# Windowed attention and feed-forward: probabilities transposed in blocks on VectorE and moved through DRAM, from the third batch on

## The chip, the core and the metric

The kernel runs on one core of a Trainium2 chip. The metric is the device time of one execution in microseconds. Five things work side by side on the core, each with an in-order queue of its own: TensorE (PE, matmuls, with its weight loads PEld), VectorE (DVE), ScalarE (ACT), GpSimd (POOL) and SyncE (SP), which issues every transfer of this kernel. A transfer is carried out by 16 shared DMA engines after SP has issued it.

## The reference, cut to what matters

```python
batch, n_heads, seq_l, seq_g, head_dim = (8, 8, 512, 32, 64)
# attention, per batch and head: 32 global queries see all 544 keys; each of the 512 local
# queries sees the 32 global keys and the local keys at most 32 positions away
s_g = scale * np.matmul(q_g, k_all.transpose(0, 1, 3, 2))
out_g = np.matmul(sm(s_g), v_all)
mask = np.abs(pos[:, None] - pos[None, :]) <= window        # window = 32
s_l = np.concatenate([s_lg, np.where(mask, s_ll, -1e9)], axis=-1)
out_l = np.matmul(sm(s_l), np.concatenate([v_g, v_l], axis=2))
x = concatenate([out_g, out_l], axis=2), heads side by side  # 8 * 544 = 4352 rows of 512
h = x @ w_in                                                 # 512 x 2048
return (h - np.tanh(h)) @ w_out                              # 2048 x 512
```

All inputs and outputs are float32.

## The kernel before, in words

**Precision.** From the second batch on every operand of a matmul is split in a rounded part and a rest (`thi` and `tlo` for the transposed probabilities, `vv` for the values, `x_hi` and `x_lo`, `ghi` and `glo`, and so on), and a product is made of the three products hi·hi, hi·lo and lo·hi. The first part of each such pair is a copy (ACT or DVE), the second a subtraction, mostly on POOL (`subtract`).

**Attention.** A head's 512 local queries are four tiles of 128; a tile needs 192 local and 32 global keys (`KC = 224`). Tiles go in two pairs. Per pair: scores into a PSUM bank (lines 733 and 734), the row's peak with the mask (738, DVE), exponential (745, ACT), reciprocal of the sum (752, 753, DVE), scaling (758, POOL) in the buffers `prob`. The product with the values needs the keys on the partitions, so each pair's probabilities are transposed on PE in four 128x128 pieces against the identity `idr` (line 918) into a PSUM bank, from which `add_keys_first` writes `thi` (line 291, ACT or DVE) and `tlo` (line 836, DVE). The product itself is line 916: eight matmuls for a pair from the third batch on (`wide`, `CFG["newb"] = 2`), four with 128 and four with 64 weight columns, twelve in the second batch. The transposes of head i are issued inside the product of head i-1, one after each quarter of it (`add_product(pair, then)`). `thi` and `tlo` exist once: head i's writes come after head i-1's product has read them.

After the product its two halves are added (`low`, line 947), and `x_hi`, `x_lo` (953, POOL) and the global rows `xg` (957) are made.

The global queries' probabilities `pg` take another way already: 32x32 blocks transposed on DVE (line 789) into `gt`, then `thi` and `tlo` (801).

**Feed-forward.** A batch's 512 local rows are one chunk of 16 steps. A step is 12 matmuls of 512 columns for the hidden layer (line 1014), tanh (1022, ACT), difference (1025, DVE), split (`ghi` line 291, `glo` line 1031 on POOL), and 12 matmuls for the output (1062). The chunk of batch b-1 runs while batch b's attention is made, two steps for a head. `x_hi` and `x_lo` exist twice, so attention is never more than a batch ahead. After the last head the last batch's chunk and one of the 256 global rows remain.

**Order.** The class `Order` lays every operation on its engine's queue at build time: a list scheduler with a price for each operation, due times (the numbers in `CFG`), and choices such as "this copy on ACT or on DVE". The queues on the chip are in order, so an operation that waits holds all behind it.

**Transfers.** For each head SP issues four loads of keys and queries (551), four moves of the keys to the score operand `kw` (646), two of the queries (651) and three loads of values (855, 866); for each batch also ten for the global keys and queries and four of the output (1090).

## Time and profile before

| | |
|---|---|
| median of three runs | 1089.13 us (1078.9 to 1089.97) |
| the profiled execution, its own time | 1082.97 us |
| span of the profile, first to last instruction | 1081.2 us |
| mean granted TensorE clock | 0.987 of full speed |
| busy: PE, DVE, ACT, POOL | 95%, 64%, 58%, 61% of the span |
| bytes moved by the DMA engines | 97.10 MB |

The span is 1.8 us shorter than the execution's own time. Busy shares are of the whole span. The program has stages: the first two batches (0 to some 221 us, with the weights being loaded and split), six batches of attention beside the feed-forward of the batch before (221 to 934 us), and a tail of feed-forward alone. A busy PE is not a PE at its peak, since matmuls overlap in the record: the pace is read from the starts of successive matmuls. Times in the lists are us from the start of the span; "idle before" is time in which the engine stood still ahead of an instruction, with what released it. Releasers named with a small q are sequencers; SPq rows are SP issuing a transfer.

### The profile page before, as it was taken

Reading aid. Unit: us, or ns where it says so; the run is one execution under the profiler, and the core shown is the slowest. Engines: PE = TensorE matmul, PEld = TensorE weight load, DVE = VectorE, ACT = ScalarE, POOL = GpSimd, SP = SyncE. Lnnn points to the kernel's source line nnn. Section 1 sums busy time; section 2 is a strip of 40 time slices with the busy share of each in tenths; the row PEclk is TensorE's granted clock in tenths of the full one; section 3 lists DMA queues with packets and bytes.
Section 4 is the critical chain, followed back from the end, with each engine's and each line's share of the span. In section 5 each row is a group of like instructions: output and inputs, shape, how many; then the busy total and the mean of one; then the engine's idle time right before and its main releaser. Section 6 shows DMA issues by size and latency. Waiting matters only on the chain.

```text
span 1081.2 us, 19499 instructions
## 1 busy us (share of the span) xinstructions
PE 1022.2 (95%) x5660; PEld 858.0 (79%) x5660; DVE 695.3 (64%) x2167; ACT 630.7 (58%) x1764; POOL 659.1 (61%) x912
## 2 busy tenths in 40 slices
PE   5987999879999899999999999999999999999997
PEld 3765878668888788878888888878888888888896
DVE  5786877777676776677666776677757776422221
ACT  4776767557674766576665766477647666311111
POOL 4556767567675677577666776677756776522221
PEclk9998999889999999999999999999999999999999
DMA  7655545454334532353334433353335331000010
GB/s 180 154 138 152 148 119 153 113 139 93 70 82 86 134 83 64 68 137 84 78 67 114 92 84 79 75 138 79 76 66 140 84 79 45 16 24 1 1 40 20
DMA packets 270795, 97.10 MB, mean 90 GB/s; under 512 B 217312, under 2 KB 255072, under 8 KB 270688
## 3 DMA queue, kind: packets, MB, share of 16 engines
q1 hardware_dynamic: 270688, 95.86, 38.5%
q8 instruction: 45, 0.74, 0.3%
q14 instruction: 62, 0.51, 0.2%
HBM read 49.27 MB, written 8.91 MB: 54 GB/s over the span
## 4 chain that ended last, share of the span: by engine, by line
PE 82%; DMA 4%; DVE 4%; issue 3%; POOL 2%; SPq 2%; ACT 1%; POOLq 0%; DVEq 0%; ACTq 0%
PE bank L1014 33%; PE bank L1062 32%; PE bank L916 6%; PE bank L918 4%; PE bank L733 3%; PE bank L734 2%; DMA wraw<-in_moe_w_out_dram 2%; DMA lo<-lo 2%; SPq L551 1%; PE bank L676 1%; PE bank L730 1%; DVE gt L789 1%; PE bank L677 0%; DVE t L1025 0%; POOL w_out_lo L372 0%
## 5 line engine op out<-in xcount | busy, mean ns | idle before, releaser
L1031 POOL TENSOR_TENSOR glo<-t,ghi 128x512 fp32r<-128x512 f32 x136 | 176.0, 1294 | 174.7 <-DVE ghi L291 82.3
L1022 ACT ACTIVATE t<-bank 128x512 f32<-128x512 f32 x136 | 81.4, 598 | 159.5 <-PE bank L1014 154.3
L1025 DVE TENSOR_TENSOR t<-bank,t 128x512 f32<-128x512 f32 x136 | 93.9, 690 | 120.5 <-ACT t L1022 117.9
L1062 PE MATMUL bank<-w_out_hi,ghi 128*128 128x512 f32 x544 | 155.0, 399 | 4.1 <-ACT ghi L291 4.1
L1062 PE MATMUL bank<-w_out_lo,ghi 128*128 128x512 f32 x544 | 154.9, 399 | 0.0
L1062 PE MATMUL bank<-w_out_hi,glo 128*128 128x512 f32 x544 | 154.4, 397 | 0.4 <-POOL glo L1031 0.4
L1014 PE MATMUL bank<-x_lo,w_in_hi 128*128 128x512 f32 x512 | 142.4, 400 | 0.0
L1014 PE MATMUL bank<-x_hi,w_in_hi 128*128 128x512 f32 x512 | 141.8, 401 | 0.0
L1014 PE MATMUL bank<-x_hi,w_in_lo 128*128 128x512 f32 x512 | 140.9, 397 | 0.0
L758 POOL TENSOR_SCALAR prob<-prob,st 128x224 f32<-128x224 f32 x240 | 107.2, 460 | 37.1 <-DVE st L753 21.8
L745 ACT ACTIVATE prob<-prob,st 128x224 f32<-128x224 f32 x240 | 113.7, 476 | 21.1 <-DVE st L738 19.8
L1062 PEld LDWEIGHTS bank<-w_out_hi,ghi 128*128 128x128 f32 x544 | 100.9, 190 | 25.8 <-ACT ghi L291 5.4
L738 DVE CUSTOM_DVE_ANT_0 prob<-bank,mask 128x224 f32<-128x224 f32 x240 | 83.2, 388 | 56.0 <-PE bank L734 53.1
L918 PE MATMUL bank<-idr,prob 128*128 128x128 f32 x440 | 116.8, 282 | 1.8 <-DVE xg L977 1.0
L916 PE MATMUL bank<-thi,vv 128*128 128x160 f32 (+5 forms) x512 | 118.3, 286 | 0.0
L1062 PEld LDWEIGHTS bank<-w_out_lo,ghi 128*128 128x128 f32 x544 | 100.3, 190 | 19.3
L1062 PEld LDWEIGHTS bank<-w_out_hi,glo 128*128 128x128 f32 x544 | 99.2, 189 | 20.3 <-POOL glo L1031 1.3
L1014 PEld LDWEIGHTS bank<-x_hi,w_in_hi 128*128 128x128 f32 x512 | 95.5, 192 | 21.3 <-ACT x_hi L291 0.6
L953 POOL TENSOR_TENSOR x_lo<-wraw,x_hi 64x256 fp32r<-64x256 f32 x96 | 70.8, 738 | 60.3 <-ACT x_hi L291 33.9
L1014 PEld LDWEIGHTS bank<-x_lo,w_in_hi 128*128 128x128 f32 x512 | 93.5, 191 | 17.6
L1014 PEld LDWEIGHTS bank<-x_hi,w_in_lo 128*128 128x128 f32 x512 | 92.6, 190 | 17.0
L916 PE MATMUL bank<-tlo,vv 128*64 128x160 f32 x448 | 104.2, 233 | 0.0
(132 smaller groups left out, 2057.9 us busy)
## 6 DMA issues: line engine op xcount, KB each, us to landing
wraw<-in_moe_w_in_dram SPq DMA_DIRECT2D x32, 256.0 KB, 3.0
wraw<-in_moe_w_out_dram SPq DMA_DIRECT2D x32, 256.0 KB, 3.1
out_dram<-wraw SPq DMA_DIRECT2D x32, 256.0 KB, 2.3
vraw<-in_v_l_dram SPq DMA_DIRECT2D x56, 128.0 KB, 2.4
raw<-in_k_l_dram SPq DMA_DIRECT2D x112, 64.0 KB, 2.3
raw<-in_q_l_dram SPq DMA_DIRECT2D x112, 64.0 KB, 2.3
hi<-hi SPq DMA_DIRECT2D x56, 128.0 KB, 2.3
lo<-lo SPq DMA_DIRECT2D x56, 128.0 KB, 2.3
```

Of the source, the lines that this page charges most:

```text
L733: nc.tensor.matmul(t_[:, i, :KC], part_lo[:, q], kw2[:, t], start=True, stop=False)
L738: nc.vector.tensor_tensor_reduce(out=self.prob[t][:, :KC], in0=getattr(self, f"s_{pair}")[:, i, :KC], in1=tile_mask[t], scale=-0.125, scal ...
L745: nc.scalar.activation(x, x, AF.Exp, bias=self.st[:, t:t + 1], scale=-1.0, accum_out=self.st[:, 4 + t:5 + t])
L758: nc.gpsimd.tensor_scalar(x, x, self.st[:, 8 + t:9 + t], 1.0, op0=ALU.mult, op1=ALU.mult)
L916: nc.tensor.matmul(dst, l, r, start=i == 0, stop=i == len(mm) - 1, skip_group_check=True)
L918: nc.tensor.transpose(*turns[i // each], idn)
L953: eng[e].tensor_sub(places()[1], view(total, [(160, 2), (1, P)]), f32(places()[0]))
L1014: nc.tensor.matmul(self.h[s][:, j * n:(j + 1) * n], w[:, cc, f * P:(f + 1) * P], self.x()[xi][:, cc, :n], start=part == 0 and cc == 0 and ...
L1022: nc.scalar.activation(tt_[q], self.h[s], AF.Tanh)
L1025: nc.vector.tensor_sub(tt_[q], self.h.pop(s), tt_[q])
L1031: eng[e].tensor_sub(gg[q][1], tt_[q], f32(gg[q][0]))
L1062: nc.tensor.matmul(self.acc[tt], g[:, j * self.n + tt * P:j * self.n + (tt + 1) * P], low_out(f) if wi else w_out_hi[:, f], start=s == 0 a ...
```

## The change

For heads of the third batch and later the transposes leave PE. `add_blocks` makes, for each pair, one DVE instruction that transposes all 32x32 blocks of the 128x512 probabilities into `turned` (line 873). That puts each block right within itself, but a block's rows stay in the 32 partitions in which they were. Four transfers (882), one for each group of 32 partitions, write `turned` to a DRAM buffer `spread` (there are two), and one transfer (886) reads it back so that the keys lie on the partitions; it lands in the second half of the one buffer `th`, which takes the place of `thi` and `tlo`. From there a copy makes the rounded part (line 310, ACT or DVE) and a subtraction in place the rest (895, POOL).

`turned` lies in two of the three buffers `wraw`, which the weights' loads and the output rows use. `th` has another layout: 32 queries of each kind side by side, so that the global queries' part of a tile is a fifth column group; the product (line 978) reads it with a stride, its bank grows from 288 to 320 columns, and the global rows' two parts are added by POOL afterwards: one addition more for the second pair (1020, 1021), and an addition in place of a copy by ACT or DVE for the first (1023).

The second batch keeps the transposes on PE; they now come after the first matmul of each quarter of the product. All numbers of the order are other ones, the offsets are now separate for the first, the second and the later batches (`PHASE`), and the scheduler's price for issuing one transfer is 0.6 in place of 0.475 us. The arithmetic and the matmuls of the feed-forward are as before.

How the order of instructions moves on PE. In the kernel before, a pair's product in a batch past the second reads (bank = PSUM, `idr` = identity):

```order
L1014 MATMUL bank_103<-x_hi_1154,w_in_lo 128x512 x4
L916 MATMUL bank_104<-thi,vv 128x160
L916 MATMUL bank_104<-tlo,vv 64x160
L918 MATMUL bank_105<-idr,prob_87 128x128
...
L1062 MATMUL bank_110<-w_out_hi,glo_74 128x512
```

After the change PE reads so, from the last rows of one head's second product to the next head's first; the three rows left out behind each L1128 are the same matmul for the other three banks:

```order
L978 MATMUL bank_107<-th,vv 128x128
L978 MATMUL bank_107<-th,vv 64x128
L1128 MATMUL bank_111<-w_out_hi,ghi_76 128x512
...
L1080 MATMUL bank_105<-x_hi_1106,w_in_hi 128x512 x4
L1128 MATMUL bank_111<-w_out_lo,ghi_76 128x512
...
L1080 MATMUL bank_105<-x_lo_1107,w_in_hi 128x512 x4
L1128 MATMUL bank_111<-w_out_hi,glo_77 128x512
...
L1080 MATMUL bank_105<-x_hi_1106,w_in_lo 128x512 x4
L1128 MATMUL bank_111<-w_out_hi,ghi_78 128x512
...
L978 MATMUL bank_107<-th,vv 128x160
```

Every L918 row between the rows of a product is gone, and seven groups of four 512-column matmuls stand between the products of these two heads. It is the narrowest of the six places of this kind inside a batch: in most batches the six hold 8, 10, 10, 8, 7 and 10 such groups, the first four of them a later head's two global-score matmuls (L692, L693) besides.

On SP, the rows of one head before:

```order
L855 DMA vraw<-in_v_l_dram 128x4x64
L855 DMA vraw<-in_v_l_dram 64x4x64
L866 DMA vraw<-in_v_g_dram 32x4x64
L646 DMA kw<-hi_82 64x2x192
L646 DMA kw<-hi_82 64x2x160
L646 DMA kw<-lo 64x2x192
L646 DMA kw<-lo 64x2x160
L651 DMA hi_82<-hi_82 64x512
L551 DMA raw_66<-in_k_l_dram 32x16x32 x2
L551 DMA raw_66<-in_q_l_dram 32x16x32 x2
L651 DMA lo<-lo 64x512
```

and after:

```order
L882 DMA spread_61<-wraw_72 32x4x256 x4
L913 DMA vraw<-in_v_l_dram 128x4x64
L913 DMA vraw<-in_v_l_dram 64x4x64
L924 DMA vraw<-in_v_g_dram 32x4x64
L662 DMA kw<-hi_85 64x2x192
L662 DMA kw<-hi_85 64x2x160
L662 DMA kw<-lo 64x2x192
L662 DMA kw<-lo 64x2x160
L886 DMA th<-spread_61 128x1024
L667 DMA hi_85<-hi_85 64x512
L571 DMA raw_70<-in_k_l_dram 32x16x32 x2
L571 DMA raw_70<-in_q_l_dram 32x16x32 x2
```

Five issues are new. The read-back (L886) waits for the landing of the four writes and for the product of the head before; the queries' moves and the next head's loads stand behind it.

The diff's core:

```diff
+    spread = [dp.tile([4, 32, 4, 256], F32, name=f"spread{j}") for j in range(2)]
...
+    wraw01 = cp.tile([P, 2, 256, 2], F32, name="wraw01")
+    wraw = [wraw01[:, 0], wraw01[:, 1], cp.tile([P, 256, 2], F32, name="wraw2")]
+    turned = wraw01.rearrange("p j n k -> p (j n k)")
...
-    thi, tlo = [Later(cp, [P, 2, 2, 320], n) for n in ("thi", "tlo")]
+    th = Later(cp, [P, 2, 5 * 2 * NT * 32], "th")
+
+    def local_part(i, pair):
+
+        return view(th()[:, i], [(128, 8), (1, 64)], 64 * pair)
...
+        def add_blocks(self):
+            half = [("wraw", 0), ("wraw", 1)]
+            for pair in range(2):
+                def turn(e, _, pair=pair):
+                    src = self.prob[2 * pair]
+                    nc.vector.transpose(view(turned, [(128, 2), (256, 4), (32, 2), (1, 32)], 64 * pair),
+                                        view(src, [(P, 2), (32, 4), (KC, 2), (1, 32)]))
+
+                add(("D", 0.72), turn, self.due(self.C["o_u"] + self.C["o_up"] * pair), r=[self.k(f"p{pair}")], w=half)
+
+            box = spread[self.i % 2]
+
+            def leave(e, _):
+                for r in range(4):
+                    nc.sync.dma_start(box[:, :, r].rearrange("g p n -> p g n"),
+                                      turned[32 * r:32 * r + 32].rearrange("p (g n) -> p g n", g=4))
+
+            def come(e, _):
+                nc.sync.dma_start(f32(th()[:, 1, :4 * 256]), box.rearrange("g p r n -> (g p) (r n)"))
...
+                def high(e, _, pair=pair):
+                    copy(e, local_part(0, pair), f32(local_part(1, pair)))
+
+                def rest(e, _, pair=pair):
+                    eng[e].tensor_sub(local_part(1, pair), f32(local_part(1, pair)), f32(local_part(0, pair)))
...
-                t_ = bank([P if wide else D, 288], tags[o])
+                t_ = bank([P if wide else D, 288 if self.plain else 320], tags[o])
...
-                    hi, lo = [x[:k, pair, a, c0:c1] for x in (thi(), tlo())]
-                    vhi, vlo = [vv()[:k, a, t, i] for i in range(2)]
+                    hi, lo = [view(th()[:, i], [(256, n), (1, 32)], a * 128 + t * 32) for i in range(2)]
+                    vhi, vlo = [vv()[:, a, t, i] for i in range(2)]
...
                 def glob(e, _):
+                    x = [total[:, c + P:c + P + G] for c in (0, 160)]
                     if pair:
-                        eng[e].tensor_add(g, total[:, P:P + G], g)
+                        eng[e].tensor_add(x[0], x[0], x[1])
+                        eng[e].tensor_add(g, x[0], g)
                     else:
-                        copy(e, g, total[:, P:P + G])
+                        eng[e].tensor_add(g, x[0], x[1])
...
+        blocks = a.b >= CFG["newb"]
         for pair in range(2):
-            heads[i - 1].add_product(pair, a)
+            heads[i - 1].add_product(pair, None if blocks else a)
+        if blocks:
+            a.add_blocks()
```

More of the change, by code (lines that the diff above doesn't have):

```diff
@@ L239 @@
     first_mask = first_qm[:, 2 * S:2 * S + 608]
-    first_t = [cp.tile([P, 2, 2, 320], F32, name=f"first_t{j}", tag=n) for j, n in enumerate(("thi", "tlo"))]
+    first_t = cp.tile([P, 2, 2, 2, 320], F32, name="first_t", tag="th")
+    first_t = [first_t[:, j] for j in range(2)]
     first_v = cp.tile([P, 2, 2, NT, D], F32, name="first_v", tag="vv")
@@ L612, in __init__ @@
                 self.kw, self.q, self.v = first_kw[self.u], first_q[self.u], first_v[:, self.two]
-            self.f = CFG["f0"] if self.b == 0 else 1.0
-        @property
-        def thi(self):
-            return first_t[self.two] if self.plain else thi()
+            self.C = PHASE[min(self.b, 2)]
         def due(self, off):
-            return base(self.i) + off * self.f - (CFG["last"] if self.b == B - 1 else 0)
+            return base(self.i) + off - (CFG["last"] if self.b == B - 1 else 0)
         def k(self, name):
@@ L932, in add_product @@
                 w = w + [(f"t{pair}", then.i)]
-            add(("T", time + (0.436 if then else 0.174 if wide else 0.0)), mm, due, r=reads, w=w, res=res,
-                alloc=alloc, rows=0.87, ldw=0.107 if wide else 0.053, tail=0.107 if then else 0.06)
+            add(("T", time + (0.45 if then else 0.0)), mm, due, r=reads, w=w, res=res,
+                alloc=alloc, rows=0.75, ldw=0.107 if wide else 0.053, tail=0.076)
             if then:
-                then.add_keys_first(pair, CFG["o_t"] + CFG["o_tpp"] * pair)
+                then.add_keys_first(pair, then.C["o_t"] + then.C["o_tpp"] * pair)
             xgk = ("xg", self.i, pair)
@@ L939, in add_product @@
                 key = slot("p")
-                raw = wraw[key[1]].rearrange("p n k -> p (n k)")[:, :288]
+                raw = wraw[key[1]].rearrange("p n k -> p (n k)")[:, :320]
                 lows, total = raw[D:], raw[rows]
@@ L1252, in xgs @@
         def xgs():
-            return [t().rearrange("p a b c -> p (a b c)")[:, :NCC * ng].rearrange("p (a c) -> p a c", a=NCC) for t in (thi, tlo)]
+            return [th()[:, i, :NCC * ng].rearrange("p (a c) -> p a c", a=NCC) for i in range(2)]
         was = [n + "0" for n in ("h0", "h1", "l0", "l1", "hg", "lg")]
```

147 lines of the change are left out of this document (86 added, 61 removed).

## The prediction

> **What bounds the kernel now.** First the page: its span, busy shares, granted clock and the shares of the chain that ended last.
>
> ```profile
> span 1081.2 us, 19499 instructions
> ...
> PE 1022.2 (95%) x5660; PEld 858.0 (79%) x5660; DVE 695.3 (64%) x2167; ACT 630.7 (58%) x1764; POOL 659.1 (61%) x912
> ...
> PEclk9998999889999999999999999999999999999999
> ...
> PE 82%; DMA 4%; DVE 4%; issue 3%; POOL 2%; SPq 2%; ACT 1%; POOLq 0%; DVEq 0%; ACTq 0%
> ```
>
> PE bounds it: 82% of the chain, 95% busy, at nearly full clock after the first quarter. Averages over stages hide what a stage is short of, so next the busy time by stage; the second to fifth row are the first two batches, two whole batches of the middle, and the tail.
>
> ```profile
> core 0: us, PE busy (x) PEld busy (x) DVE busy (x) ACT busy (x) POOL busy (x), PEclk, DMA share, GB/s
> 0.00:221.40 221.40, 186.70 (x1017) 150.47 (x1017) 170.27 (x587) 149.11 (x438) 139.11 (x206) 0.95 0.58 145
> 460.30:578.80 118.50, 115.10 (x654) 97.24 (x653) 82.79 (x255) 76.03 (x214) 80.16 (x113) 1.00 0.41 90
> 578.80:697.80 119.00, 116.31 (x662) 98.69 (x661) 83.10 (x255) 78.51 (x218) 81.78 (x115) 1.00 0.41 90
> 934.40:1081.20 146.80, 141.38 (x715) 119.66 (x713) 30.41 (x56) 21.96 (x39) 36.95 (x32) 1.00 0.05 19
> ```
>
> A middle batch takes 118.7 us; PE is idle 3.0 of them, POOL 38, DVE 36, ACT 41. Six such batches are what the change touches. Work taken off PE there is time, as long as no other queue takes PE's place.
>
> **What the change takes off PE.** The list of PE's instructions in order of time shows the same product with and without transposes, since the last head has nobody's transposes to carry.
>
> ```profile
> 924.34 0.23 PE L916 MATMUL bank<-thi,vv 128*128 128x160 f32 x1
> 924.41 0.24 PE L916 MATMUL bank<-tlo,vv 128*64 128x160 f32 x1
> 924.48 0.27 PE L918 MATMUL bank<-idr,prob 128*128 128x128 f32 x1
> ...
> 925.29 1.17 PE L1014 MATMUL bank<-x_hi,w_in_lo 128*128 128x512 f32 x4
> 926.30 1.08 PE L1062 MATMUL bank<-w_out_hi,ghi 128*128 128x512 f32 x4
> 927.22 1.08 PE L1014 MATMUL bank<-x_hi,w_in_hi 128*128 128x512 f32 x4
> ...
> 933.76 0.23 PE L916 MATMUL bank<-thi,vv 128*128 128x160 f32 x1
> ...
> 934.42 1.15 PE L1062 MATMUL bank<-w_out_lo,ghi 128*128 128x512 f32 x4
> 935.40 0.24 PE L916 MATMUL bank<-thi,vv 128*128 128x160 f32 x1
> ```
>
> With transposes a pair holds PE from 924.34 to 925.29, 0.95 us, and the group behind it takes 1.01 us (to 926.30) where a group otherwise takes 0.92. Without, 933.76 to 934.42 is 0.66 us and the group behind takes 0.98. The difference is 0.29 + 0.03 = 0.32 us a pair. The change does it for 48 heads of two pairs: 96 x 0.32 = **30.7 us**. The durations that the record gives a transpose (0.27) would make it three times as much, but those overlap; the starts count. The stride with which the product now reads `th`, and its bank's 32 further columns, are in no row; nearest is that the 160-column and 128-column matmuls read strided halves already, so 0, with 0 to 5% of 0.66 us (3 us) as bounds.
>
> [...]
>
> **What it adds, and where that lies.** Rows of groups by line (count, busy us, mean ns, idle before):
>
> ```profile
> L1031 POOL TENSOR_TENSOR glo<-t,ghi 128x512 fp32r<-128x512 f32 x136 | 176.0, 1294 | 174.7 <-DVE ghi L291 82.3 <-PE bank L1062 62.3 <-ACT ghi L291 8.3
> L953 POOL TENSOR_TENSOR x_lo<-wraw,x_hi 64x256 fp32r<-64x256 f32 x96 | 70.8, 738 | 60.3 <-ACT x_hi L291 33.9 <-DVE x_hi L291 13.5 <-ACT xg L291 9.1
> L957 POOL TENSOR_TENSOR xg<-wraw,xg 64x32 f32<-64x32 f32 x48 | 12.0, 250 | 5.0 <-DVE wraw L947 3.6
> L836 DVE TENSOR_TENSOR tlo<-bank,thi 128x512 fp32r<-128x512 f32 x112 | 77.0, 687 | 6.9 <-ACT thi L291 5.0
> L555 DVE STREAM_TRANSPOSE kq<-raw 128x512 f32<-128x512 f32 x56 | 39.7, 710 | 10.1 <-POOL lo L564 7.6 <-DMA kw<-hi 1.4
> L291 DVE CAST ghi<-t 128x512 fp32r<-128x512 f32 x79 | 38.7, 490 | 14.2 <-PE bank L1062 8.0
> L291 ACT CAST vv<-vraw 128x512 fp32r<-128x512 f32 x54 | 33.4, 618 | 0.2
> L291 DVE CAST hi<-kq 128x512 fp32r<-128x512 f32 x4 | 1.7, 415 | 0.0
> ```
>
> DVE loses two `tlo` (687 ns) and gains two block transposes, by the transpose of the same size 710 ns: even. ACT copies `th` where it copied `thi`, two copies of 512 columns a head (0.62 us, as `vv`): even. Both keep over 30 us idle a batch; that idle time hides it, and 0 is taken. POOL gains, a head, two subtractions (2 x 1.29) and two small additions (2 x 0.25): 3.1 us, so a batch goes from 80.2 to 80.2 + 24.7 = **105 us** of POOL, against a PE that would need 115.1 - 16 x 0.32 = 110. POOL keeps about a tenth idle and is the cover that goes thin. PE's waits on POOL are one row today; I take 0.5 us a batch, **3 us**, and keep 0 to 31 as bounds (the upper end is a rival).
>
> SP issues 118 transfers a batch by the code, and 40 more after. Issues and landings in their views:
>
> ```profile
> 613.29 0.55 SPq L651 DMA_DIRECT2D lo<-lo  x1
> 621.10 1.29 SPq L646 DMA_DIRECT2D kw<-hi  x2
> ```
>
> ```profile
> wraw<-in_moe_w_in_dram SPq DMA_DIRECT2D x32, 256.0 KB, 3.0
> ...
> hi<-hi SPq DMA_DIRECT2D x56, 128.0 KB, 2.3
> ```
>
> ```profile
> PE bank L733 <- DMA lo<-lo: 7.8, 8, 2.7
> ...
> PE bank L1062 <- POOL glo L1031: 0.4, 1, 0.4
> ```
>
> At 0.55 to 0.65 us each, 0.6 in the mean, 118 issues are 71 us and 158 are 95 of some 114 us a batch. SP stands idle for 7 us at a time today (613.84 to 621.10), which hides the issues themselves.
>
> The new **wait** is a loop through the one buffer `th`. After a head's last product: read-back, copy, subtraction, next product. The read-back is 512 KB, which no row shows; from 128 KB to 256 KB the landing grows by 0.7, so 512 KB is 3.0 + 1.4 = 4.4 us as an estimate. With 0.62, 1.29 and half an SP issue (0.3) before it is taken up, the loop is 6.6 us, and with one POOL instruction of 1.3 already running 7.9. In PE's new order the six places between two heads' products hold 6.4 (seven groups of 0.92), twice 7.6, twice 9.5 and 9.2 us of work (608 columns of global scores are 0.27 at the groups' pace, 0.92 for 2048). A 6.6 us loop stalls PE 0.2 us a batch, a 7.9 us loop 1.5 + 0.3 + 0.3 = 2.1. I take 7.9, since POOL will rarely be free: 6 x 2.1 = **12.6 us**; bounds 1 and 65 (last rival). While the read-back waits on SP, the queries' moves and the next head's loads wait behind it, and behind those the scores (L733 on `lo<-lo`, 7.8 us today); the next head's scores stand at least a product ahead in need, so nothing is added for it.
>
> The reordering of the first two batches keeps their work. PE idles 34.7 of their 221.4 us, so there is room both ways; a quarter of it, 8.7 us, is the bound, and 0 the value.
>
> **Sum.** 1083.0 (profiled execution) - 30.7 + 12.6 + 3.0 = 1067.9, so **1068 us**. That execution lies 6 us below the median of the runs shown, inside their spread; the forecast is in its terms.
>
> **Rivals.**
>
> *Full gain.* The read-back lands by 3.1 us, or POOL is free when it does; loop and POOL cost nothing: 1083.0 - 30.7 = 1052. For it: POOL's and ACT's operations are ordered around the new arrivals. Against: 6.4 us of cover is just the loop with nothing in its way.
>
> *POOL takes the bound.* POOL's 105 us need 13.7 us idle in a batch, 1.7 a head, to fill today's 118.7; then nothing is gained: 1083. For it: in the rows above POOL waits 0.63 us before each `x_lo`, two a head, and 1.28 before each `glo`, two a head, 3.8 in all. Against: most of those waits are slack, time in which nothing was asked of it. DVE's `ghi` casts took 490 ns in the mean. [...]
>
> *The read-back is late, slower than before.* One place: line 886. If it lands 6.6 us after its issue, or SP reaches it 2.2 us late, the loop is 10.1 us and the six places stall 3.7 + 2.5 + 2.5 + 0.6 + 0.6 + 0.9 = 10.8 us a batch, 65 in all: 1083.0 - 30.7 + 65 = 1117. It decides from a landing of 5.9 us on: loop 9.4, stalls 6.8 a batch, 41 us, 1% over today. For it: SP at 95 of 114 us, and a DMA share that is 0.41 in the middle before this adds 1 MB a head. Against: the share leaves the engines half free, and three places of six have over 9 us.
>
> *The transposes cost PE nothing now*, so removing them gains nothing: 1083. Against: the 0.29 us between the two products above, at the same clock.
>
> **Chances.** A measurement here tells 1% (11 us) from no change. Forecast, 1058 to 1078: 0.42, of which 0.30 under 1072. Full gain: 0.22. POOL bound: 0.17. Late read-back: 0.17. Transposes free: 0.02. Faster by over 1%: 0.30 + 0.22 + 0.03 of the POOL case (a part of the gain left) = 0.55. Slower by over 1%: 0.17 + 0.02 of the POOL case (with the pair's exclusion) = 0.19. Within 1%: 0.26. The range runs from 1048, full gain with a little from the first batches, to 1104, halfway into the late case; beyond lie about 0.05 and 0.14. The forecast's own is 1058 to 1078.
>
> **What would show it.** Right: PE's count falls by 384, a product takes 0.66 us at its starts, POOL's busy time in a middle batch is 104 to 106 us, and a middle batch takes about 116 us. In the waits PE stands before line 978 for POOL's line 895, about 2 us a batch, most at the place with seven groups. Wrong: a product slower than 0.70 us (the stride costs); line 886 landing after 5.9 us or PE waits of over 7 us a batch before 978; POOL idle under 5 us a batch with PE waiting for `glo`; or a change of over 9 us before 221 us, which is the order and not the transposes.

## The result and the profile after

The changed kernel takes 1099.36 us in the median of four runs (1094.49 to 1104.5), beside 1084.24 us for the kernel before on the same chip: a ratio of 1.0161, with a 95% interval of 1.0123 to 1.0199. The forecast was 1068; the time moved the other way. Single executions of two experiments were disturbed (2456 and 5320 us); comparisons leave them out, and the profile of the first experiment below, which fell on one, is not read. The kernel before had a median of 1079 to 1084 us beside the different experiments, so kernels are compared by their ratios to it; 1% is 10.8 us.

The page of the changed kernel's profile (its execution took 1101.26 us): busy time, granted clock, chain that ended last.

```profile
PE 1013.7 (92%) x5276; PEld 830.2 (76%) x5276; DVE 719.5 (65%) x2172; ACT 640.5 (58%) x1743; POOL 794.6 (72%) x1104
...
PEclk9779999899999999999999999999999899999999
...
PE 36%; POOL 18%; DMA 16%; DVE 9%; issue 8%; SPq 6%; ACT 6%; POOLq 0%; DVEq 0%; ACTq 0%
PE bank L1128 14%; PE bank L1080 12%; DMA th<-spread 6%; PE bank L978 5%; POOL th L895 3%; DMA wraw<-in_moe_w_out_dram 3%; POOL lo L584 3%; POOL glo L1097 2%; POOL vv L930 2%; POOL prob L774 2%; ACT th L310 2%; POOL x_lo L1015 2%; SPq L571 2%; DVE st L768 1%; DVE gt L805 1%
```

PE has 384 instructions fewer, but its share of the chain fell from 82% to 36%: POOL and the transfers, the read-back first among them, took its place. Busy time by stage, two middle batches:

```profile
464.00:586.00 122.00, 114.37 (x594) 93.90 (x593) 85.28 (x248) 79.39 (x214) 104.27 (x147) 0.99 0.66 157
586.00:712.00 126.00, 115.64 (x594) 95.00 (x593) 84.14 (x247) 79.09 (x215) 103.62 (x145) 0.97 0.63 151
```

VectorE and ScalarE are where they were, POOL has its 104 us as worked out, and yet a batch takes 122 to 126 us where it took 118.7. The best measure is from head 16's global scores to head 56's, five batches without start and tail (the columns are span, busy time and count of PE, PEld, DVE, ACT and POOL, granted clock, DMA share, GB/s). First the kernel before, then the changed one:

```profile
221.36:814.68 593.32, 576.68 (x3265) 488.54 (x3265) 414.27 (x1275) 382.66 (x1073) 402.60 (x562) 0.99 0.41 90
```

```profile
219.59:832.41 612.82, 570.64 (x2981) 468.66 (x2980) 429.76 (x1245) 398.11 (x1073) 519.32 (x723) 0.99 0.65 156
```

PE stands 42.2 us there (612.8 - 570.6) where it stood 16.6, and its busy time fell by 6.0 us only. The two stretches do not hold quite the same work, since the new order has done more of the feed-forward when it comes to head 56's global scores. One of the three kinds of output matmul, before and after:

```profile
L1062 PE MATMUL bank<-w_out_hi,ghi 128*128 128x512 f32 x312 | 88.5, 398 | 0.0
```

```profile
L1128 PE MATMUL bank<-w_out_hi,ghi 128*128 128x512 f32 x320 | 93.1, 405 | 13.1 <-ACT ghi L310 12.5 <-ACT wraw L310 0.7
```

With the other two kinds that is 24 matmuls of 512 columns more after the change, and 16 product matmuls more (664 for 648): some 6.8 us by their starts (6 x 0.92 + 2 x 0.66). For the same work PE's busy time so fell by about 12.8 us, and the five batches took about 12.7 us longer, not 19.5. The stands are not touched by this. What PE waited for in that stretch, the two largest rows before, then the changed kernel (total, times, longest):

```profile
PE bank L733 <- DMA lo<-lo: 4.6, 6, 1.5
PE bank L733 <- DVE wraw L947: 4.2, 4, 1.5
```

```profile
PE bank L1128 <- ACT ghi L310: 12.5, 6, 2.7
PE bank L692 <- DMA kw<-lo: 8.1, 4, 3.1
PE bank L749 <- DMA lo<-lo: 7.7, 11, 1.4
PE bank L978 <- POOL th L895: 3.4, 9, 0.5
```

The wait that the prediction priced, L978 for L895, is the smallest of these four. The largest two come about once a batch, at its last head (hidden values) and its third (the score operand `kw`), and were not there before. Two places in PE's order, one ordinary product and one such stand:

```profile
533.52 0.83 PE L978 MATMUL bank<-th,vv 128*128 128x160 f32 x8
534.19 1.15 PE L1080 MATMUL bank<-x_hi,w_in_hi 128*128 128x512 f32 x4
...
568.68 2.08 PE L1128 MATMUL bank<-w_out_hi,ghi 128*128 128x512 f32 x4 [2.20 <-ACT ghi L310]
570.56 1.46 PE L978 MATMUL bank<-th,vv 128*128 128x160 f32 x8
571.84 1.15 PE L1128 MATMUL bank<-w_out_lo,ghi 128*128 128x512 f32 x4
```

By its starts a product takes 0.67 us (533.52 to 534.19). Behind the stand of 2.20 us a group takes 1.88 (568.68 to 570.56) instead of 0.92, and a product 1.28: about 3 us at half pace. The granted clock is on record as half from 568.5 to 571.9. This stand so cost 2.20 us and 1.58 more, nearly double its length.

What comes late at the third head is in the chain in order of time:

```profile
600.96 0.46 SPq L886
601.51 0.59 SPq L662
602.15 3.69 DMA kw<-lo
606.08 0.66 PE bank L692
```

The copy to `kw` is issued right behind the 512 KB read-back and lands after 3.69 us; 2.2 was the median before. Landings over the whole run (KB, median us), one row of the kernel before, then the changed one:

```profile
raw<-in_k_l_dram SPq DMA_DIRECT2D x112, 64.0 KB, 2.3
```

```profile
th<-spread SPq DMA_DIRECT2D x48, 512.0 KB, 3.9
...
raw<-in_k_l_dram SPq DMA_DIRECT2D x112, 64.0 KB, 3.3
...
hi<-hi SPq DMA_DIRECT2D x56, 128.0 KB, 3.3
```

`raw` and `hi`, the next head's loads and moves behind the read-back, took 2.3 us each before. The medians of the copies to `kw` hardly moved (2.1 to 2.3 us): they are late at single places.

### The profile page after: what moved, and what is told of

Same layout as the page of the kernel before. It is cut to its first block, busy times and chain, and to the rows that moved or that the text cites. A ratio compares the mean times of both kernels' runs of the same rounds, so it can differ in the third digit from the quotient of the medians.

```text
span 1099.3 us, 19237 instructions
## 1 busy us (share of the span) xinstructions
PE 1013.7 (92%) x5276; PEld 830.2 (76%) x5276; DVE 719.5 (65%) x2172; ACT 640.5 (58%) x1743; POOL 794.6 (72%) x1104
## 4 chain that ended last, share of the span: by engine, by line
PE 36%; POOL 18%; DMA 16%; DVE 9%; issue 8%; SPq 6%; ACT 6%; POOLq 0%; DVEq 0%; ACTq 0%
PE bank L1128 14%; PE bank L1080 12%; DMA th<-spread 6%; PE bank L978 5%; POOL th L895 3%; DMA wraw<-in_moe_w_out_dram 3%; POOL lo L584 3%; POOL glo L1097 2%; POOL vv L930 2%; POOL prob L774 2%; ACT th L310 2%; POOL x_lo L1015 2%; SPq L571 2%; DVE st L768 1%; DVE gt L805 1%
## 5 line engine op out<-in xcount | busy, mean ns | idle before, releaser
L1091 DVE TENSOR_TENSOR t<-bank,t 128x512 f32<-128x512 f32 x136 | 92.3, 680 | 135.1 <-ACT t L1088 133.9
L1128 PE MATMUL bank<-w_out_hi,ghi 128*128 128x512 f32 x544 | 157.6, 404 | 18.7 <-ACT ghi L310 18.0
L1128 PE MATMUL bank<-w_out_lo,ghi 128*128 128x512 f32 x544 | 152.5, 394 | 0.0
L1128 PE MATMUL bank<-w_out_hi,glo 128*128 128x512 f32 x544 | 152.4, 394 | 0.0
L1128 PEld LDWEIGHTS bank<-w_out_hi,ghi 128*128 128x128 f32 x544 | 100.3, 191 | 43.8 <-ACT ghi L310 23.0
L895 POOL TENSOR_TENSOR th<-th 128x512 fp32r<-128x512 f32 x96 | 123.2, 1291 | 10.6 <-ACT th L310 7.8
L978 PEld LDWEIGHTS bank<-th,vv 128*128 128x128 f32 (+1 forms) x960 | 105.5, 163 | 23.7 <-POOL th L895 9.7
L978 PE MATMUL bank<-th,vv 128*128 128x160 f32 (+2 forms) x960 | 111.2, 258 | 8.1 <-POOL th L895 3.9
L1128 PEld LDWEIGHTS bank<-w_out_lo,ghi 128*128 128x128 f32 x544 | 100.4, 189 | 19.8
L1128 PEld LDWEIGHTS bank<-w_out_hi,glo 128*128 128x128 f32 x544 | 99.3, 188 | 19.7
L1080 PEld LDWEIGHTS bank<-x_lo,w_in_hi 128*128 128x128 f32 x512 | 97.6, 195 | 21.2 <-DVE x_lo L1037 0.8
L1080 PEld LDWEIGHTS bank<-x_hi,w_in_hi 128*128 128x128 f32 x512 | 92.9, 189 | 25.2 <-DVE t L1091 4.4
L754 DVE CUSTOM_DVE_ANT_0 prob<-bank,mask 128x224 f32<-128x224 f32 x240 | 80.8, 387 | 18.1 <-PE bank L750 15.7
L805 DVE STREAM_TRANSPOSE gt<-pg 32x160 f32<-32x160 f32 x224 | 73.2, 327 | 19.0 <-POOL th L818 11.6
```

The lines of the kernel that those rows point to most:

```text
L754: nc.vector.tensor_tensor_reduce(out=self.prob[t][:, :KC], in0=getattr(self, f"s_{pair}")[:, i, :KC], in1=tile_mask[t], scale=-0.125, scal ...
L805: nc.vector.transpose(gt[r, :c], view(pg[e0:e0 + 32, 32 * q:32 * q + 1], [(P, c), (1, 32)]))
L895: eng[e].tensor_sub(local_part(1, pair), f32(local_part(1, pair)), f32(local_part(0, pair)))
L978: nc.tensor.matmul(dst, l, r, start=i == 0, stop=i == len(mm) - 1, skip_group_check=True)
L1080: nc.tensor.matmul(self.h[s][:, j * n:(j + 1) * n], w[:, cc, f * P:(f + 1) * P], self.x()[xi][:, cc, :n], start=part == 0 and cc == 0 and ...
L1091: nc.vector.tensor_sub(tt_[q], self.h.pop(s), tt_[q])
```

## The experiments

Theory A: POOL, busy 104 of 122 us in one order, hands over late. Theory B: the transfers make others late. Theory C: the new written order itself costs the time. Where an edit doesn't say otherwise, every engine keeps its order.

### The subtractions moved, the transfers shrunk, both left out, both moved

`e1`: the two subtractions on VectorE.

```
-                    eng[e].tensor_sub(local_part(1, pair), ...)
+                    nc.vector.tensor_sub(local_part(1, pair), ...)
```

> The changed kernel with one edit: the two in-place subtractions of a head (L895, 1.29 us each on POOL) are given to VectorE, at the same place of the written order; PE, ACT and SP keep every instruction in its order. It takes 8 x 2 x 1.29 = 20.6 us of the 104 off POOL in each middle batch, which is then near the 80 us of the kernel before, and puts some 11 us on VectorE, which has 40% of the time free. Theory A (POOL late: with 104 of 122 us busy in one order it is behind at the change of batches, and x, the hidden values and the next heads' keys come late): most of the 15 us by which the change is slower goes, 1078 to 1086 us, and PE's waits at L1128, L692 and L749 shrink. Theory B (transfers late: the read-back and the four writes of a head in SP's one queue, and their bytes on the rings, make the copies to kw and lo late): only the 4 us of waits at L895 go, 1093 to 1100 us. Theory C (the new order itself, drawn from the new table of numbers, costs the time): 1095 to 1100 us.

Measured: 1104.95 us, ratio 1.020 (1.015 to 1.026). No gain. As POOL was relieved, theory A seemed to fall; the run was not a clean one, as the later ones show.

`e2`: 32 KB for 512.

```
-   dma_start(box[:, :, r] ..., turned[32 * r:32 * r + 32] ...)
+   dma_start(box[0, :8, r], turned[32 * r:32 * r + 8, :256])
-   dma_start(f32(th()[:, 1, :1024]), box ...)
+   dma_start(f32(th()[:8, 1, :1024]), box[0, :8] ...)
```

> The changed kernel with all five transfers of a head still issued, but each cut to one sixteenth of its bytes (32 of 512 KB either way), so most of the low half of the probabilities stays from earlier heads and the output is not the attention of these inputs. Every engine keeps its instructions in their order. Theory B with the bytes as the cause (DMA share 0.65 where it was 0.41, landings of the other copies 0.3 to 1.0 us longer): the copy to kw lands in 2.2 us again, PE's 12 us of waits at L692 and 9 us at L749 in the middle fall to the 5 us that the kernel before had, and the half clock behind them goes: 1068 to 1080 us. Theory B with the issues as the cause, Theory A and Theory C: 1090 to 1100 us, as the issues, POOL and the order stay.

`e3`: `leave` and `come` issue nothing.

> The changed kernel without the five transfers: the transposes by blocks, the copies and the subtractions stay, and the low half of the probabilities is never fetched, so the output is not the attention of these inputs. SP loses 5 issues a head (40 of 158 a batch) and its waits at L886 (18.3 + 9.2 us in the middle), the rings 1 MB a head, and the loop through the read-back is gone. Theory B: all that the transfers cost comes back and the PE saving of 30.7 us shows against the kernel before: 1052 to 1066 us. Theory A: POOL still has its 104 us a batch, so only the 4 us of waits at L895 and part of the waits at L749 go: 1086 to 1096 us. Theory C: 1088 to 1098 us.

`e4`: the edits of `e1` and `e3`.

> The changed kernel with both edits: the in-place subtractions on VectorE and no transfers (the low half of the probabilities is never fetched, so the output is not the attention of these inputs). What is left of the change is the PE saving, the VectorE transposes, the ACT copies and the new order. Theories A and B in any mixture: the whole saving shows, 1050 to 1058 us (1083.0 - 30.7 = 1052.3 by the prediction's term). Theory C: the stalls at the change of batches stay, 1078 us or more.

Measured: `e2` 1084.07 us, ratio 1.0051 (1.0014 to 1.0088); `e3` 1087.24 us, 1.0037 (1.0002 to 1.0072); `e4` 1094.16 us, 1.0123 (1.0058 to 1.0187). The transfers cost 1.24% or 13.4 us (1.0161 to 1.0037), and all of it goes with their bytes: the five issues with a sixteenth of the bytes cost no more than none that shows. But against the 1052 us of the full gain some 35 us are still missing. `e4` came out slower than `e3`, though their intervals touch: the subtraction seems to suit VectorE no better than POOL. A row of `e4` that goes with it:

```profile
L895 DVE TENSOR_TENSOR th<-th 128x512 fp32r<-128x512 f32 x96 | 88.3, 922 | 4.7 <-ACT th L310 3.1
```

It takes 922 ns on the mean, where VectorE's difference of 512 columns at L1091, which reads one operand from a bank, takes 680. So taking work from POOL had to be tried without giving it to anyone.

### POOL's work cut, alone and with the transfers gone

```
-   eng[e].tensor_sub(local_part(1, pair), f32(local_part(1, pair)), ...)
+   nc.gpsimd.tensor_sub(local_part(1, pair)[:, :1], f32(local_part(1, pair)[:, :1]), ...)
```

> The changed kernel with each in-place subtraction on POOL (L895) cut from 512 to 64 columns: by the 64x32 subtractions of 0.24 us and the 64x256 of 0.73 us it takes some 0.3 us and not 1.29, so POOL has 16 us a batch less (104 to 88), and no other engine gets them (giving them to VectorE had put waits for ACT's copies into VectorE's order). Seven eighths of the low half stay unsubtracted, so the output is not the attention of these inputs. All transfers and all orders stay. Theory A (POOL late): the hand-overs behind POOL come earlier, 1080 to 1088 us. Theory B (the bytes of the transfers, which by the run with small transfers cost 15 us): 1094 to 1100 us. Theory C (the order): 1094 to 1100 us.

> The changed kernel without the five transfers and with the POOL subtractions cut to 64 columns (neither the low half's fetch nor most of its subtraction is done, so the output is not the attention of these inputs). Without the transfers alone it took 1087 us, with PE idle 6.9 us a middle batch. Theory A: the stands at L978 for L895 (6.3 us in five batches) and at L1128 for ACT's copies that follow POOL (8.9 us) go with the half clock behind them, 1062 to 1074 us. Theory C (the written order puts products and hidden steps too close behind what they wait for, whatever POOL does): 1080 to 1088 us.

Measured: `e5` 1080.29 us, ratio 0.999 (0.9955 to 1.0025); `e6` 1053.61 us, ratio 0.9767 (0.9735 to 0.9799). The same five batches in `e3`, `e5` and `e6`, one row of each:

```profile
211.42:815.21 603.79, 569.83 (x2981) 469.74 (x2980) 422.94 (x1245) 398.70 (x1074) 520.31 (x723) 0.99 0.41 88
```

```profile
212.40:810.09 597.69, 563.86 (x2982) 468.19 (x2981) 424.99 (x1245) 398.27 (x1073) 444.36 (x724) 0.99 0.67 160
```

```profile
214.28:790.84 576.56, 557.93 (x2981) 465.50 (x2980) 423.25 (x1245) 396.89 (x1074) 444.04 (x724) 1.00 0.43 93
```

With POOL at 444 and not 519 us and the transfers gone, the change's own order gives most of the full gain, 1053.6 us; theory C, the order as the cost by itself, falls. Each part alone gives back less than half:

| | ratio | against the changed, % | five batches, us | PE busy | PE standing |
|---|---|---|---|---|---|
| before | 1 | | 593.3 | 576.7 | 16.6 |
| changed | 1.0161 | | 612.8 | 570.6 | 42.2 |
| no transfers | 1.0037 | -1.24 | 603.8 | 569.8 | 34.0 |
| subtractions cut | 0.9990 | -1.71 | 597.7 | 563.9 | 33.8 |
| both | 0.9767 | -3.94 | 576.6 | 557.9 | 18.6 |

The row before holds some 6.8 us of PE's work less than the others, as said above; those four hold the same. The columns in us are of one execution each; the ones without transfers and with the subtractions cut took 8.5 and 6.1 us less than the medians of their kernels.

POOL's work costs 1.71% (18.5 us) with the transfers there and 2.70% (29 us) without them; the transfers 1.24% (13.4) and 2.23% (24). Together 42.6 us: 10.7 of them, give or take 8 by the four intervals, go only when both go. Cutting the subtractions also shortens the loop from read-back to product, but PE's waits at L978 fell by only 5 us in five batches (5.9 to 0.8). Note the column PE busy: the same matmuls in the same order take 12.7 us less in the last row than in the second. A part is the half pace behind the stands: the granted clock is on record as half for 13.7 us of the second row's stretch and for 3.4 of the last's, so 6.8 and 1.7 us were lost to it. That is 5.1 of the 36 us between these rows, a seventh; the rest of the 12.7 is not explained.

In `e6` PE's waits shrink at L1128, L692 and L749; at L978 they stay (5.9 us in both, in fewer and longer stands):

```profile
PE bank L978 <- DVE st L704: 5.6, 5, 1.7
PE bank L749 <- DMA lo<-lo: 4.0, 4, 1.3
PE bank L1128 <- ACT ghi L310: 3.5, 6, 0.6
PE bank L692 <- DMA kw<-lo: 2.1, 2, 1.7
```

ScalarE's wait named at L1128 fell from 12.5 to 3.5 us, although only POOL and the transfers were touched: ScalarE, which PE waits for last, must itself have waited further up.

### Doses in the kernel before

```
 eng[e].tensor_sub(vv()[:, :, :, 1], vraw, ...)        # and behind L801
+for _ in range(5 if self.b >= 2 else 0): nc.gpsimd.tensor_sub(dose, f32(dose), f32(dose))
```

> The kernel before with a dose of POOL work: from the third batch on five subtractions of 128x24 on a tile of their own behind each head's subtraction of the global probabilities and five behind that of the values, some 0.24 us each, 2.4 us a head, 19 us a batch: as much as the change's two subtractions. Nobody waits for them, and every other instruction stays in its order. Theory A: POOL at 99 of 119 us in one order hands over late as in the changed kernel, 1090 to 1100 us. Theories B and C: POOL has the room, 1080 to 1085 us.

```
+for r in range(4): dma_start(spread[i % 2][:, :, r] ..., f32(w_out_hi[32 * r:32 * r + 32, 0:2]) ...)
+dma_start(spread[2 + i % 2] ..., spread[(i + 1) % 2] ...)      # behind the last copy of the queries
```

> The kernel before with a dose of transfers: from the third batch on four writes of 128 KB a head from constant weights to DRAM, behind the loads of the values, and one copy of 512 KB, DRAM to DRAM, of what the head before wrote, behind the last copy of the queries: the change's bytes and issues on the same queue, without its loop, since nobody waits for their result. All other instructions stay in their order. Theory B: the copies to kw and lo land later as in the changed kernel (2.2 to 3.7 us at worst), PE's waits at L676 and L733 grow from 15 us to 30 us or so, 1090 to 1098 us. Theories A and C: 1080 to 1085 us.

Measured: `e7` 1116.65 us, ratio 1.035 (1.030 to 1.040); `e8` 1142.55 us, ratio 1.060 (1.052 to 1.067). Both came out far above what was expected. In `e7` five batches hold 487.49 us of POOL where they held 402.60, 17 us a batch that nobody waits for, and take 621.8 us in place of 593.3: 5.7 us a batch. POOL's 38 idle us a batch in the kernel before were no free room for work. The whole dose cost 3.5% or 37.6 us, more than the change's POOL work (18.5 to 29). In `e8` the waits of PE over five batches are these two before all:

```profile
PE bank L734 <- issue: 20.5, 9, 3.3
PE bank L734 <- DMA lo<-lo: 16.9, 10, 3.4
```

The scores wait for their copies, though the median landings are those of the kernel before (`raw` and `hi` 2.3 us): this run shows no slower landing of these copies, and by which step they come late was not settled. This dose is no measure of what the change's transfers cost (13 to 24 us), since the order of the kernel before was made without such transfers.

### Writes alone, read-back alone

`e9`: `come` issues nothing. `e10`: `leave` for the first two heads only.

> The changed kernel without the read-back: the four writes of a head stay, the low half of the probabilities is never fetched, so the output is not the attention of these inputs. All orders stay. Without any of the five transfers it took 1087 us, with all of them at a sixteenth of their bytes 1084 us, as it is 1099 us. Theory B1 (the 512 KB read-back, in front of the copies to kw and lo in the one queue, makes them late): most of the 12 to 15 us comes back, 1084 to 1090 us. Theory B2 (the four writes, 4 of the 5 issues, do): 1094 to 1100 us.

```
-                for r in range(4):
+                for r in range(4 if self.i < 2 * H + 2 else 0):
```

> The changed kernel with the four writes issued for the first two heads of the third batch alone: every head reads back 512 KB as before, but the content of those two heads, so the output is not the attention of these inputs. All orders stay. Theory B1 (the read-back makes the copies to kw and lo late): 1094 to 1100 us. Theory B2 (the writes do): 1084 to 1090 us. If each costs its share of the bytes: 1089 to 1094 us.

Measured: `e9` 1086.63 us, ratio 1.0053 (1.0020 to 1.0085); `e10` 1100.31 us, 1.0200 (1.0160 to 1.0240). The 512 KB that are read back in one transfer cost everything; the same 512 KB written in four cost nothing that shows. With the writes alone `raw` and `hi` land after 2.3 us, with the read-back alone after 3.2. A read-back in four pieces was not tried, so the one piece and the direction are not told apart.

### POOL's multiplications given to VectorE and to ScalarE

```
-   nc.gpsimd.tensor_scalar(x, x, self.st[:, 8 + t:9 + t], 1.0, ...)
+   (nc.vector if self.b >= 2 else nc.gpsimd).tensor_scalar(x, x, ...)
```

> The changed kernel with the four multiplications of a head's local probabilities by the inverse sums (L774, 0.44 us each on POOL) given to VectorE from the third batch on, right behind the reciprocal that VectorE computes for them; nothing is left out. POOL has 14 us a batch less (104 to 90), VectorE some 13 us more (78 to 91 of 122), and a hand-over between the two engines is gone. Theory A (POOL late, worth 19 us by the run with the subtractions cut): 1080 to 1088 us. If VectorE in its order is then as late as POOL was (as with the subtractions on it, 1105 us): 1095 to 1106 us.

> The kernel before with the same edit: the multiplications of the local probabilities on VectorE from the third batch on, nothing left out. POOL has 14 us a batch less (80 to 66). The dose of 17 us a batch on POOL had cost 37 us in that kernel. If the time follows POOL on both sides of 80 us: 1055 to 1070 us. If PE is the bound there, as the prediction has it (idle 3.6 us of a middle batch), little is to be had: 1074 to 1084 us. If VectorE's order suffers: 1086 us or more.

```
-   nc.gpsimd.tensor_scalar(x, x, self.st[:, 8 + t:9 + t], 1.0, ...)
+   nc.scalar.activation(x, x, AF.Copy, scale=self.st[:, 8 + t:9 + t])      # third batch on
```

> The changed kernel with the multiplications of the local probabilities (L774, 0.44 us each on POOL) on ScalarE from the third batch on, as a copy with a scale; nothing is left out. POOL has 14 us a batch less (104 to 90), ACT some 14 more, by its 0.47 us for 128x224 (75 to 89 of 122). Theory A (POOL late): 1080 to 1090 us. If ACT's order, which now stands for VectorE's reciprocal ahead of the hidden values, is as late as POOL was: 1098 us or more.

Measured: in the changed kernel 1135.5 us on VectorE, ratio 1.054 (1.048 to 1.059), and 1110.05 us on ScalarE, 1.029 (1.025 to 1.033); in the kernel before, on VectorE, 1097.94 us, 1.017 (1.014 to 1.020). All three are slower. The multiplication on VectorE in the changed kernel, then in the kernel before:

```profile
L774 DVE TENSOR_SCALAR prob<-prob,st 128x224 f32<-128x224 f32 x192 | 109.9, 613 | 1.5
```

```profile
L758 DVE TENSOR_SCALAR prob<-prob,st 128x224 f32<-128x224 f32 x192 | 69.7, 405 | 2.3
```

The same instruction takes 613 ns beside 452 us of POOL work in five batches and 405 beside 333. The two kernels differ otherwise too. In none of these tries did relieving POOL help when another engine took the work.

### Where the read-back does its harm

`e13` puts the read-back behind the copies to `kw` in SP's order where they stand next to it; `e14` issues it from ScalarE's queue.

```
-   nc.sync.dma_start(f32(th()[:, 1, :4 * 256]), ...)
+   nc.scalar.dma_start(f32(th()[:, 1, :4 * 256]), ...)
```

> The changed kernel with one edit in SP's order: where copies to kw stand as one of the next two transfers behind a head's read-back (L886), the read-back goes behind them. All other orders stay, nothing is left out. It saves the kw copies the wait behind 512 KB at the head after a change of batch, where PE stood 12.0 us at L692 for kw<-lo in the middle, and delays the read-back by some 1.4 us at those heads. If the place ahead of kw is the harm: 1086 to 1093 us. If it is the bytes on the rings, or what stands behind the read-back in every head (the next head's raw and hi, which land after 3.3 us where they took 2.3): 1096 to 1102 us.

> The changed kernel with the read-back issued by ScalarE and not by SP, at the same place of the written order; nothing is left out. The copies behind it no longer follow 512 KB in their own queue, and SP no longer stands at L886 (18.3 + 9.2 us in the middle); the bytes still go over the same 16 engines. ACT now stands there for the writes to land and for the last product, with exponentials and hidden values behind it, and has 40% of the time free. If the one queue is the harm and ACT's waits cost little: 1080 to 1090 us. If the bytes on the rings are: 1095 to 1102 us. If ACT's waits decide: 1105 us or more.

Measured: `e13` 1120.16 us, ratio 1.036 (1.031 to 1.041); `e14` 1100.42 us, 1.019 (1.014 to 1.023). In `e13`, over the five batches, the wait for `kw` shrinks and the products wait instead (the first row names the engine that the record shows last; with L895 and the like the waits at L978 are 23 us, where they were 6):

```profile
PE bank L978 <- DVE st L704: 18.6, 13, 3.7
PE bank L1128 <- ACT ghi L310: 15.8, 10, 2.3
PE bank L749 <- DMA lo<-lo: 6.1, 6, 1.4
PE bank L692 <- DMA kw<-lo: 3.3, 1, 3.3
```

So the place ahead of `kw` did matter, but the other place matters more: some 1.2 us later (two issues) at a part of the heads cost 20 us. Read-back and `kw` seem both urgent at that moment, and whichever goes second is late. `e14`'s landings:

```profile
th<-spread ACTq DMA_DIRECT2D x48, 512.0 KB, 4.1
...
raw<-in_k_l_dram SPq DMA_DIRECT2D x112, 64.0 KB, 3.4
...
hi<-hi SPq DMA_DIRECT2D x56, 128.0 KB, 3.3
```

On a queue of its own (q10 of this profile, 25.17 MB) the read-back delays SP's transfers just as much, `raw` and `hi` by 1 us, and PE's waits at L692 for `kw` grow (15.9 us in eight, where they were 8.1 in four). So on both queues that were tried the transfer itself delays them, and not its place in SP's queue.

### Two hand-overs tried alone

`e16` and `e17` leave out one instruction of VectorE; `e18` does too, and moves copies on ScalarE behind the next instruction there.

```
-   nc.vector.tensor_scalar(self.st[:, a:a + n], self.st[:, a:a + n], 1e-9, None, op0=ALU.add)
```

> The changed kernel without VectorE's addition of 1e-9 to the local sums (L768). Each sum holds the exponential of 0 of its row's greatest score, so it is at least 1, and in single precision the addition changes no bit. Everything else stays in its order. In the changed kernel's profile this instruction on 128x2 takes 473 ns on the mean and up to 1845 ns, where the reciprocal of the same size behind it takes 166 ns, because it ends only when POOL's running instruction ends; 16 a batch stand between exponential and multiplication. Theory A by this way (POOL's work stops VectorE in the softmax chains): 1082 to 1092 us. If POOL does its harm through its own order alone: 1096 to 1101 us.

> The kernel before without the same addition (L752, 296 ns on the mean there, up to 1259), which changes no bit of the sums. PE is idle 3.6 us of a middle batch. If the waits for POOL cost time there too: 1070 to 1077 us. If PE is the bound: 1077 to 1083 us.

> The changed kernel without the addition, and with each copy of the read-back's halves that stands on ScalarE moved behind the next instruction of ScalarE's order, where nothing between needs it; nothing else is moved. ScalarE stood 35.4 us at these copies in the middle (40 times, up to 2.1 us), and an instruction of some 0.4 to 0.6 us now runs in that time. If ScalarE's stand is the read-back's harm: 5 to 10 us below the run without the addition. If the products, which wait for the copies, are: 5 us or more above it.

Measured: `e16` 1099.7 us, ratio 1.018 (1.013 to 1.023); `e17` 1080.59 us, 1.001 (0.999 to 1.004); `e18` 1100.57 us, 1.022 (1.019 to 1.026). None gains. That VectorE's addition stops for POOL in the softmax chains is real (84 of 97, last section), but this one hand-over is not how POOL's work costs time. Nor does `e6` remove it: the addition takes 463 ns there where it took 473. `e18` settles less: from 220 to 925 us ScalarE stands 30.9 us at its copies, where it stood 50.8 in `e16`, but PE's waits at L978 grow from 2.4 to 13.5 us. Whether that stand is how the read-back costs time stays open.

## Why the prediction was wrong, point by point

**PE's saving, 30.7 us: right for PE's work.** A product takes 0.66 to 0.67 us at its starts. For the same work PE's busy time in five batches is 25.6 us less in `e6` than before (576.7 + 6.8 - 557.9), and 80 pairs at 0.32 are 25.6. In the time 25 us of it arrive (22 to 29): `e6` takes 0.9767 of the time before, 1058 us in the prediction's terms, where the rival of full gain said 1052. `e6` keeps 41 us of added POOL work in five batches; that this holds back the rest is not shown. The new layout, its stride and the wider bank cost nothing that shows. What PE got rid of was worth some 0.3 us a pair, and the loss lies in POOL's work and the round trip.

**VectorE and ScalarE even, 0: right.** Their work in a middle batch moved by some 2 us, and `e6`, which has the gain, keeps it all.

**POOL, 3 us: the largest error.** Its busy time came out as worked out (104 us), its price did not: 18.5 us with the transfers there, 29 without them, within the bound of 31 us that the prediction left to a rival. The failed step is "PE's waits on POOL are one row today; I take 0.5 us a batch". PE's waits show who came last, and POOL's delay reached PE under other names (L1128 for ScalarE's `ghi` fell from 12.5 to 3.5 us with POOL and the transfers relieved). `e7` shows that POOL's idle time was no cover. The rival in which POOL takes the bound, 1083, is near what remains with the transfers gone: `e3`, 1087 us. No run shows that POOL and VectorE's casts shut each other out, the "pair's exclusion" behind the 0.02 for a slower outcome of it; in the profile before, five of VectorE's 79 `ghi` casts (L291), begun while POOL worked at `vv` (L872), took 1.39 to 1.50 us, and the other 74 took 0.42 to 0.43, with POOL at work beside 16 of them.

**The loop, 12.6 us: the size near by luck, the place wrong.** The read-back lands after 3.9 us, estimated 4.4, and PE stands before L978 for L895 3.9 us in the whole run, not 12.6. The transfers cost 13.4 us nevertheless, 24 with POOL relieved, but by other waits. The late rival (1117 us, from a landing of 5.9 us on) did not come about in the change; `e13` issued the read-back some 1.2 us later at a part of the heads and took 1120 us; the rival had 2.2 us at every head and 65 us of waits at L978, where `e13` has 23 in five batches, so the likeness of the times is luck.

**The transfers around it, 0: wrong.** The failed step is "the next head's scores stand at least a product ahead in need, so nothing is added for it". I had counted SP's issues, which indeed cost nothing (`e2`, `e9`), and looked at the DMA share, 0.41, which seemed to leave room (it became 0.65). What the runs show in its place is a delay of transfers near the read-back, 1 us for `raw` and `hi`, 1.5 for `kw` at the place above, and PE's waits for `kw`, 8.1 us in five batches, at heads where nothing was in hand. How the cost divides between this delay and the read-back's own late landing at its copies no run separates.

**The clock, not in the sum at all.** Full clock was read as given. Behind some stands PE ran at half pace, and 5.1 of the 36 us that the two costs take in five batches are this.

**The first two batches, 0: right.** They end at 219.6 us, where they ended at 221.4; in single executions of the other runs that keep this stage this end lies between 211 and 227 us.

By its own terms: 1083.0 - 30.7 = 1052.3, and the two costs together are 42.6 us where 15.6 were taken; that gives 1095, and the saving's missing 5.5 us make it the measured 1.0161.

Open: by which hand-overs POOL's work reaches PE. Its own subtractions' waits at L978 are too small, and VectorE's stop at L768 is without effect when taken away. No version that leaves nothing out beat the kernel before.

## What to carry to other kernels

Test work on an engine off the critical path with a dose of the same work that nobody waits for, and do not price it by its idle share or by the waits that name it: 17 us a batch into 38 idle ones cost 5.7. The dose warns, but its cost is not the price: here it came out at 37.6 us where the change's POOL work cost 18.5 to 29, and for the transfers at 6% where theirs cost 1 to 2. Price a large transfer by what the transfers issued beside it lose (here 1 us each for `raw` and `hi`), and two small costs together rather than one by one, because each uses the slack on which the other's price was based. And where a matmul engine stands for two microseconds, look whether it runs slowly afterwards: here one stand of 2.20 us cost 1.58 more.

## What the runs showed of the hardware that was not expected

**VectorE's small addition ended with POOL's instruction.** The addition on 128x2 and the reciprocal of the same size, changed kernel, groups by line; then one of them on VectorE, and POOL beside it:

```profile
L768 DVE TENSOR_SCALAR st<-st 128x2 f32<-128x2 f32 x128 | 60.6, 473 | 6.2 <-ACT prob L761 4.9
L769 DVE RECIPROCAL st<-st 128x2 f32<-128x2 f32 x128 | 21.3, 166 | 4.4
```

```profile
480.59 0.98 DVE L768 TENSOR_SCALAR st<-st 128x2 f32<-128x2 f32 x1
481.60 0.17 DVE L769 RECIPROCAL st<-st 128x2 f32<-128x2 f32 x1
```

```profile
480.25 1.29 POOL L1097 TENSOR_TENSOR glo<-t,ghi 128x512 fp32r<-128x512 f32 x1
```

The addition ends at 481.57, some 25 ns after POOL's subtraction (481.54), and so do most of those that begin while POOL works (84 of 97 within 60 ns); the 128 reciprocals took 165 to 169 ns each, 45 of them begun while POOL worked. What the addition's wait is worth in time was not found by taking away L768.

**Half pace behind stands of 2 to 4 us.** In the middle of the changed kernel the four stands of over 2.7 us (2.73, 2.81, 3.07 and 3.86) are each followed by three to five us in which a matmul of 512 columns starts 427 ns after the one before, and not 227; the record has the granted clock at half there, 3.4 us or 6.8 at a time. Of the stands between 1.4 and 2.2 us some are (2.20 at 568.68) and others are not (1.97 at 447.19).
